# Threshold attention and an MLP mixer on one core: scores of two units per visit in six PSUM banks, everything else in two

## The chip, the cores and the metric

The kernel runs on 1 core of one Trainium2 chip. The metric is the device time of one execution in microseconds (us). Engines are named as in the profile: PE is TensorE (PEld its weight loads), DVE is VectorE, ACT is ScalarE, POOL is GpSimd, SP is SyncE, which here only issues DMAs. ACT issues DMAs as well, from the same instruction queue that it computes from. PSUM is the memory that PE writes to, eight banks of 128 partitions x 512 fp32 values.

## What is computed

```
batch, heads, seq, head_dim = 8, 8, 576, 64      d_model 512, d_tok 256, d_ch 1536, all fp32
scores = q @ k.T / 8
thresh = max(scores, -1) - tau                    (tau 0.02)
scores = where(scores >= thresh, scores, -1e9)
attn   = softmax(scores)                          (+1e-9 in the denominator)
x      = attn @ v, heads side by side             (8, 576, 512)
u      = x + (relu(x^T @ w_tok1) @ w_tok2)^T      mixing of tokens
out    = u + relu(u @ w_ch1) @ w_ch2              mixing of channels
```

The inputs come as 64-bit words where they are float64; the weights are converted to fp32 on the chip.

## The kernel before

**Units.** The attention of one batch row (called a row here, b = 0 to 7) has four pairs of heads. Two pairs make nine units of 128 queries each (the fifth shares its partitions between both pairs), so a row has UB = 18 units, and the program 144. A unit goes through: `scores` (L311: for each head of the pair two matmuls of 288 keys; they write a tile `sc` of two banks per head), a maximum per head on DVE (L316), the bias from it on POOL (L317), then `weigh`: the threshold as a Prelu on ACT out of PSUM (L326, "the mask" below) and the exponential with its sum in place (L333); then `norm`: 1/sum on DVE (L340, L341) and the multiplication on POOL (L344); then, two units later, `turn_blocks`: one 32x32-block transpose on DVE (L372), and after every third unit sixteen DMAs on SP that put the blocks in their places (L381, `eT<-T`). `values` (L416, L421: 20 or 40 matmul records into one bank, copied out by ACT at L425) follows three units after the third unit. Row 0 uses PE transposes through PSUM (`turn`, L360) in place of the blocks and DMAs.

**Loads.** q and k of the next pairs come in by DMAs on ACT's queue from row 1 on (`load_qk`, L109). The buffers `lq` and `lk` exist once. A load may start when `prep` (L293, two DVE block transposes, `qT<-lq` and `kT<-lk`) has read the pair before. `prep` stands at units t = 2 and 7 of every nine, the loads that follow it at t = 3, 4, 5, 6 and at 8, 0, 1, so at least one unit later.

**The MLP.** When a row's last values are done, `push(b)` puts its steps into the list `todo`: five transposes of x (`turn_x`, L450, copied out by ACT at L451), two `tok1` (L457, Relu on ACT at L459), eight `tok2` (L467, added to x on DVE at L471), and for each 256 tokens twelve `ch1` (L510, Relu on ACT at L511) and eight `ch2` steps (L531, four parts that add up in one bank for 128 tokens, then an add on DVE at L543 and the store at L550). Every step has a cost in the planner's us. `fill(share)` is called five times per unit and lets so much work out as a share of `quota`, the row's sum less KEEP (20, 45 for the last but one row) over 17 units. What is kept is done in the next row, between the first steps of that row. Rows 1 to 6 do half of their channel MLP in this way, and the rest is spilled and done at the end, as row 7's, by a product of seven block multiplications (`class Late`, L834) over five groups.

**PSUM.** `ps_sc` has two tiles of two banks (the two heads of one unit); `ps_tr` two banks for transposes and values; `ps_mm` two banks, from row 1 on, for `tok1`, `tok2`, `ch1` and `ch2`. In row 0 a third `sc` tile, `ps_3rd`, takes the place of `ps_mm`.

**Weights.** 31 pieces are loaded by SP into four raw buffers in turn and converted in steps by ACT (L206, L208), DVE (L216, L218, L222) and POOL (L230). `weight(n)` lets n of 94 steps out; `need(i)` lets out all up to piece i. In row 1 a unit has 9 steps, 12 as long as row 0's transposes are left.

The order on each engine is that in which the Python program writes the instructions; each engine runs its own in that order.

```
            if t == 2:
                prep(n + 1)
            if t == 7:
                prep(n + 2)
```

These lines stand after the loads of the same unit.

Of the kernel before, what the change touches and what calls it, by code (L numbers as in the profile page):

```python
# [21 lines left out]
def kernel(  # L22
# [52 lines left out]
    ps_sc = attn.enter_context(tc.tile_pool(name="ps_sc", bufs=2, space=bass.MemoryType.PSUM, side="right"))  # L75
    dram = ctx.enter_context(tc.tile_pool(name="dram", bufs=1, space=bass.MemoryType.DRAM))
    ps_tr = ctx.enter_context(tc.tile_pool(name="ps_tr", bufs=2, space=bass.MemoryType.PSUM))


    late = ctx.enter_context(ExitStack())  # L80
    ps_3rd = late.enter_context(tc.tile_pool(name="ps_3rd", bufs=1, space=bass.MemoryType.PSUM))
    ps_mm = None
# [65 lines left out]
    scratch = att.tile([P, GU * 4 * NK * 32], U32, tag="eT", name="scratch")  # L148
    extra = const.tile([P, 2 * WMAX], U32, name="extra")
    NRAW = 4  # L150

    high = work.tile([P, GR // P, 4, NCC * 32], F32, tag="ut", bufs=1, name="high").rearrange("q n a x -> q (n a x)")
    raw_at = [scratch[:, 2 * WMAX * i : 2 * WMAX * (i + 1)] for i in range(NRAW - 1)] + [extra]
# [28 lines left out]
    def load_piece(i):  # L182
        if i >= len(pieces):
            return
        dst, src = pieces[i]
        rows = dst.shape[0]
        n = 1
        for d in dst.shape[1:]:
            n *= d
        raw = raw_at[i % NRAW][0:rows, 0 : n * (2 if wide(i) else 1)].bitcast(src.dtype)  # L190
        nc.sync.dma_start(out=like(raw, dst), in_=src)
        if wide(i):
            words = raw.bitcast(U32).rearrange("p (n w) -> p n w", w=2)
            h2 = high[0:rows, WMAX * (i % 2) : WMAX * (i % 2) + n]
            raws[i] = like(words[:, :, 0], dst), like(words[:, :, 1], dst), like(h2, dst)
        else:
            raws[i] = like(raw, dst)
# [149 lines left out]
    def turn(u, third):  # L347
# [9 lines left out]
        ps = ps_tr.tile([P, MAIN], F32, tag="tr", name=f"tr{third}_{u}")[:, 0 : 3 * P].rearrange("p (c x) -> p c x", c=3)  # L357
# [40 lines left out]
    def values(b, p0, g):  # L398

        if b not in xTs:  # L400
            xTs[b] = work.tile([P, NP, S], F32, tag="xT", name=f"xT_{b}")
        eT = eTs.pop((b, p0, g))
        whole = ps_tr.tile([P, MAIN], F32, tag="tr", name=f"pv_{b}_{p0}_{g}")
# [28 lines left out]
    def token_mlp(b, ps=range(NP)):  # L432
# [8 lines left out]
        def psum(name):  # L441
            return (ps_mm or ps_tr).tile([P, DM], F32, tag="mm" if ps_mm else "tr", name=name)

        def turn_x(t, n):
            M = MT[t]
            to = ps_tr.tile([P, MAIN], F32, tag="tr", name=f"tx_{b}_{t}_{ps[0]}")[0:M, 0 : n * L * P].rearrange("p (t c x) -> p t c x", t=n, c=L)
# [6 lines left out]
        def tok1(m):  # L453
            need(2)
            to = psum(f"t1_{b}_{m}_{ps[0]}")[:, 0 : P * L]
            for t in range(NT):
                nc.tensor.matmul(to, lhsT=w1[:, t, P * m : P * m + P], rhs=x_sb[:, t, cols], start=(t == 0), stop=(t == NT - 1))  # L457
            if ps_mm:
# [4 lines left out]
        def tok2(c, f):  # L463
            need(6)
            to = psum(f"t2_{b}_{c}_{f}")[:, 0:HS]
# [19 lines left out]
    def channel_mlp(b, uT, i):  # L485
# [17 lines left out]

        def ch1(j):
# [3 lines left out]
            ps = ps_mm.tile([P, GR], F32, tag="mm", name=f"c1_{b}_{i}_{j}")[:, 0:n]  # L508
# [3 lines left out]
            if j == 1:  # L512
                s["us"] = work.tile([P, GR // P, 4, NCC * 32], F32, tag="us", bufs=1, name=f"us_{b}_{i}")
                if b:
                    s["ut"] = work.tile([P, GR // P, 4, NCC * 32], F32, tag="ut", bufs=1, name=f"ut_{b}_{i}")
                    turn_u()

        def ch2(t, part):
            need(7 + NJ + 3 * part + 2)
            t0 = GR * i + P * t  # L520
            if part == 0:
                s["ps"] = ps_mm.tile([P, NCC, P], F32, tag="mm", name=f"c2_{b}_{i}_{t}")
# [16 lines left out]
            if part == 3:  # L539
                o = s["us"][:, t].rearrange("q a x -> q (a x)")  # L540
                if b:
                    move_u()
# [7 lines left out]
                nc.sync.dma_start(out=out[b, t0 : t0 + P, :], in_=o)  # L550
# [5 lines left out]
    def move_u():  # L556
        while moves:
            moves.popleft()()

# [15 lines left out]
    KEEP = 20.0  # L575
    KEEP_FIRST = 20.0
    KEEP_LAST = 45.0
    todo = deque()
    quota = 0.0
    credit = 0.0  # L580

    def fill(share):
        nonlocal credit
        credit += share * quota
        while todo and credit > 0:
            cost, step = todo.popleft()
            credit -= cost
            step()
        if not todo:
            credit = 0.0  # L590


    early = deque()

    def push(b):
        nonlocal quota
        uT = xTs[b]
# [6 lines left out]
        for i, step in enumerate(steps):  # L604
            n = 2 if i in waits else 1
            todo.extend(old[:n] + [step])
            del old[:n]
        todo.extend(old)
        if b < B - 1:
            todo.append((0.0, lambda: kept.append(b)))  # L610
        for i in range(NOW[b]):
            todo.extend(channel_mlp(b, uT, i))
        quota = (sum(c for c, _ in todo) - (KEEP_FIRST if b == 0 else KEEP_LAST if b == B - 2 else KEEP)) / (UB - 1)
# [28 lines left out]
    for u in range(len(units) + LAG + 5):  # L642
        on = u < len(units)
        if u == UB:
            late.close()
            ps_mm = ctx.enter_context(tc.tile_pool(name="ps_mm", bufs=2, space=bass.MemoryType.PSUM))
        if on:
            b_now, p0, t = units[u]
            n = b_now * NP + p0
        w = u - LAG  # L650
        back = 0 <= w < len(units)
        if on:
            scores(u)
# [3 lines left out]
        if due and not in_blocks(due[0][1]):  # L657
# [4 lines left out]
        if 0 < u <= len(units):  # L662
# [3 lines left out]
        turns_left = b_now and back and not in_blocks(units[w][0])  # L666
        if b_now:
            if turns_left:
                weigh(u)
            else:  # L670
                weight(3)
        else:


            weight_to(2.25 * (u - (1 if visit else 1.5)))
            if visit:
                weigh(u)
        while copies:
            copies.popleft()()
        if last and u < UB:  # L680
            early.extend(token_mlp(0, range(NP // 2))[0])
        elif last:
            push(0)
        if back:
            wb, wp, wt = units[w]
            if not in_blocks(wb):
                for i in range(3):
                    turn(w, i)
            if wt % GU == GU - 1:
# [3 lines left out]
                due.append((u + (3 if in_blocks(wb) else 1), wb, wp, g))  # L693
        if b_now:
            fill(0.4)
        if back and in_blocks(wb):
            turn_blocks(w)
        if b_now:
            weight(6 if turns_left else 3)
        if turns_left:  # L700
            fill(0.6)
        elif on and (b_now or not visit):
            weigh(u)
        elif b_now:
            fill(0.6)
        if b_now:
            weight(3)
        elif u == 0:
# [4 lines left out]
        if on:  # L713


            when = {3: (2, 0, 2), 4: (2, 2, 4), 5: (2, 4, 6), 6: (2, 6, 8), 8: (3, 0, 3), 0: (1, 3, 6), 1: (1, 6, 8)}
            if u == 0:
                load_qk(1, (nc.sync, nc.sync), range(0, 3))
            if t in when:
                m, lo, hi = when[t]  # L720
                if n + m < len(pairs):
                    load_qk(n + m, (nc.scalar if b_now else nc.sync,) * 2, range(lo, hi))
            if t in (3, 7) and n + 2 + t // 4 < len(pairs):
                load_v(n + 2 + t // 4)
            if t == 2:
                prep(n + 1)
            if t == 7 and n + 2 < len(pairs):
                prep(n + 2)
        if due and in_blocks(due[0][1]):
            values_due(u)  # L730

        if back and wt % GU == 0 or not on:
            move_u()
# [278 lines left out]
```

## Time and profile before

| | us |
|---|---|
| median of 3 runs (1410.24 to 1419.52) | 1413.34 |
| the profiled execution | 1407.55 |
| its span | 1405.8 |
| PE busy | 1290.4 (92%) |
| DVE, ACT, POOL busy | 734.3, 592.9, 374.7 |
| unit 18, the first of row 1, starts its scores | 99.2 |
| unit 126, the first of row 7 | 837.9 |
| first matmul of the last stage (L834) | 1031.6 |

A row of the profile's groups gives busy time and the mean of one instruction, then the idle time of the engine just before such instructions and what ended it. An fp32 matmul stands there as two records. "PEclk" and "granted clock" are the share of TensorE's full clock that was granted; matmuls take longer in proportion.

### The profile page before, as it was taken

Reading aid. Unit: us, or ns where it says so; the run is one execution under the profiler, and the core shown is the slowest. Engines: PE = TensorE matmul, PEld = TensorE weight load, DVE = VectorE, ACT = ScalarE, POOL = GpSimd, SP = SyncE. Lnnn points to the kernel's source line nnn. Section 1 sums busy time; section 2 is a strip of 40 time slices with the busy share of each in tenths; the row PEclk is TensorE's granted clock in tenths of the full one; section 3 lists DMA queues with packets and bytes.
Section 4 is the critical chain, followed back from the end, with each engine's and each line's share of the span. In section 5 each row is a group of like instructions: output and inputs, shape, how many; then the busy total and the mean of one; then the engine's idle time right before and its main releaser. Section 6 shows DMA issues by size and latency. Waiting matters only on the chain.

```text
span 1405.8 us, 18371 instructions
## 1 busy us (share of the span) xinstructions
PE 1290.4 (92%) x6190; PEld 866.9 (62%) x6190; DVE 734.3 (52%) x1297; ACT 592.9 (42%) x1285; POOL 374.7 (27%) x710
## 2 busy tenths in 40 slices
PE   7886599999799989999998998898989999999998
PEld 5554365645554655564474465446658888888887
DVE  6879755446555645655564464554134443434342
ACT  6766454455555645555454454561111110202020
POOL 4565533233333323333333232330000101010100
PEclk8998899999999999999999999999999999999999
DMA  6535645646776676567566667645011110121011
GB/s 118 124 88 145 177 98 128 133 102 146 139 145 143 130 158 127 130 137 151 127 137 131 136 142 144 132 101 136 6 47 29 60 31 31 30 60 31 31 30 30
DMA packets 310574, 144.90 MB, mean 103 GB/s; under 512 B 210065, under 2 KB 303249, under 8 KB 310481
## 3 DMA queue, kind: packets, MB, share of 16 engines
q1 hardware_dynamic: 182768, 127.84, 39.1%
q10 hardware_dynamic: 127712, 15.90, 7.4%
q8 instruction: 49, 0.80, 0.3%
q14 instruction: 45, 0.36, 0.1%
HBM read 47.32 MB, written 13.50 MB: 43 GB/s over the span
## 4 chain that ended last, share of the span: by engine, by line
PE 80%; DVE 6%; DMA 5%; SPq 4%; ACT 2%; issue 1%; POOL 1%; ACTq 0%; DVEq 0%; POOLq 0%
PE c L531 11%; PE sc L311 11%; PE c L510 10%; PE o L834 9%; PE pv L421 8%; PE hx L834 6%; PE t L457 4%; PE t L467 4%; PE hz L834 4%; PE oz L834 4%; PE hmm L834 4%; PE pv L416 3%; SPq L381 2%; DMA eT<-T 2%; DVE mx L316 2%; DMA lq<-in_q_dram 1%
## 5 line engine op out<-in xcount | busy, mean ns | idle before, releaser
L316 DVE TENSOR_REDUCE mx<-sc 128x1 f32<-128x576 f32 x288 | 204.6, 750 | 331.5 <-PE sc L311 330.3
L326 ACT ACTIVATE e<-sc,bias 128x576 f32<-128x576 f32 x288 | 200.4, 740 | 135.3 <-POOL bias L317 128.3
L311 PE MATMUL sc<-kT,qT 64*128 64x288 f32 (+1 forms) x1280 | 206.5, 441 | 32.4 <-ACT e L326 31.3
L317 POOL TENSOR_SCALAR bias<-mx,toff 128x1 f32<-128x1 f32 x288 | 82.2, 286 | 565.9 <-DVE mx L316 510.0
L333 ACT ACTIVATE e<-e,ntau 128x576 f32<-128x576 f32 x288 | 220.8, 772 | 0.0
L344 POOL TENSOR_SCALAR e<-e,rr 128x576 f32<-128x576 f32 x288 | 216.5, 765 | 12.9 <-DVE rr L341 2.0
L510 PE MATMUL c<-xT,wc 128*128 128x256 f32 x768 | 182.7, 390 | 10.2 <-ACT g L511 9.1
L311 PEld LDWEIGHTS sc<-kT,qT 64*128 64x128 f32 (+1 forms) x1280 | 112.8, 180 | 124.8 <-ACT e L326 62.2
L531 PE MATMUL c<-wc,g 128*128 128x512 f32 x384 | 178.0, 604 | 0.0
L372 DVE STREAM_TRANSPOSE T<-e 128x1152 f32<-128x1152 f32 x126 | 172.0, 1365 | 7.2 <-DMA eT<-T 3.4
L510 PEld LDWEIGHTS c<-xT,wc 128*128 128x128 f32 x768 | 144.2, 193 | 46.9 <-issue 15.2
L421 PE MATMUL pv<-eT,lv 128*64 128x384 f32 (+1 forms) x1024 | 144.1, 424 | 0.0
L915 POOL TENSOR_TENSOR us<-us,ut 128x256 f32<-128x256 f32 x27 | 22.4, 845 | 411.6 <-DVE us L756 411.6
L531 PEld LDWEIGHTS c<-wc,g 128*128 128x128 f32 x384 | 70.1, 193 | 76.5 <-issue 75.9
L421 PEld LDWEIGHTS pv<-eT,lv 128*64 128x64 f32 x1024 | 79.4, 144 | 55.4 <-issue 49.7
L467 PE MATMUL t<-w,a 128*128 128x288 f32 x256 | 75.1, 431 | 10.7 <-DVE xT L471 10.7
L425 ACT COPY xT<-pv 128x384 f32<-128x384 f32 (+1 forms) x56 | 21.0, 400 | 136.6 <-PE pv L421 125.4
L416 PE MATMUL pv<-eT,vl 128*64 128x384 f32 (+1 forms) x256 | 49.5, 459 | 30.6 <-DMA eT<-T 29.5
L457 PE MATMUL t<-x_sb,w 128*128 128x512 f32 (+1 forms) x180 | 75.1, 565 | 0.0
L511 ACT ACTIVATE g<-c 128x256 f32<-128x256 f32 x96 | 36.8, 383 | 87.0 <-PE c L510 80.0
L467 PEld LDWEIGHTS t<-w,a 128*128 128x128 f32 x256 | 46.9, 194 | 36.1 <-DVE xT L471 16.8
L880 ACT ACTIVATE ga<-hmm 128x256 f32<-128x256 f32 x30 | 11.5, 384 | 123.6 <-PE hmm L834 123.6
(111 smaller groups left out, 1523.5 us busy)
## 6 DMA issues: line engine op xcount, KB each, us to landing
eT<-T SPq DMA_DIRECT2D x672, 108.0 KB, 2.3
lv<-in_v_dram SPq DMA_DIRECT2D x32, 288.0 KB, 4.0
scratch<-in_moe_w_ch_dram SPq DMA_DIRECT2D x18, 512.0 KB, 4.1
out_dram<-us SPq DMA_DIRECT2D x32, 256.0 KB, 2.0
ut<-us SPq DMA_DIRECT2D x256, 32.0 KB, 1.9
lk<-in_k_dram ACTq DMA_DIRECT2D x109, 72.0 KB, 3.1
lq<-in_q_dram ACTq DMA_DIRECT2D x106, 72.0 KB, 2.5
spill<-xT SPq DMA_DIRECT2D x6, 640.0 KB, 4.1
```

Source lines behind the costliest of these rows:

```text
L311: nc.tensor.matmul(sc[h][rows, f, 0:HS], lhsT=qT[r, cols], rhs=kT[r, HS * f : HS * f + HS], start=True, stop=True)
L316: nc.vector.tensor_reduce(out=mx[:, c], in_=sc[h][:, :, 0:HS], axis=AX.XY, op=ALU.max)
L326: nc.scalar.activation(out=eh, in_=sc[h][:, :, 0:HS], func=AF.Prelu, bias=bias[:, h : h + 1], scale=SCALE, alpha=STEEP)
L333: nc.scalar.activation(out=eh, in_=eh, func=AF.Exp, bias=ntau, accum_out=rs[:, h : h + 1])
L344: nc.gpsimd.tensor_scalar(out=eh, in0=eh, scalar1=rr[:, h : h + 1], scalar2=1.0, op0=ALU.mult, op1=ALU.mult)
L372: nc.vector.transpose(out=T[:, :, place, :].rearrange("p a (c x) -> p c a x", c=NK), in_=e.rearrange("p (c a x) -> p c a x", c=NK, a=4))
L421: nc.tensor.matmul(to[r], lhsT=lv[:, j, :], rhs=e[j], start=False, stop=(c == NI - 1), skip_group_check=True)
L457: nc.tensor.matmul(to, lhsT=w1[:, t, P * m : P * m + P], rhs=x_sb[:, t, cols], start=(t == 0), stop=(t == NT - 1))
L467: nc.tensor.matmul(to, lhsT=a[:, m, P * c : P * c + P], rhs=w2[:, m, HS * f : HS * f + HS], start=(m == 0), stop=(m == NTK - 1))
L510: nc.tensor.matmul(ps, lhsT=wc1[:, j, c, :], rhs=uT[:, c, GR * i : GR * i + n], start=(c == 0), stop=(c == NCC - 1))
L531: nc.tensor.matmul(flat, lhsT=s["g"][:, j, P * t : P * t + P], rhs=wc2[:, j, :], start=(j == 0 and b > 0), stop=(j == NJ - 1), skip_group_ ...
L834: nc.tensor.matmul(ps, lhsT=l, rhs=r, start=start and x == 0, stop=x == len(pairs) - 1, skip_group_check=not start)
```

## The change

Row 0 is kept as it was, in a loop of its own. After it all its PSUM pools are closed, and the other rows run in rounds of two units. The scores of both units go to two tiles of three banks (one per head), so that each bank holds 192 keys of the first unit and 192 of the second; 12 matmuls of 192 columns take the place of two times four of 288. All other users share the two banks left, in turn; a bank in which a `ch2` is adding up is skipped. The masks of both units now come before their exponentials, with MLP steps let out between them. The values come at the end of a round, two rounds after their unit. `prep` now stands ahead of the loads of the same unit, and the loads of both units stand ahead of the first mask. `fill` fills up to a share of a round's `quota`, in which scores (2.35) and values (4.2) are counted; `finish` does what is left of the row two before. Weights have three raw buffers in other places and seven steps a round in row 1. Stores of results are issued at the start of the next round. In the last stage, sums of weights and inputs are moved ahead, between the last steps of the rows.

```diff
+    def bank(name, hold=False):
+        if not banks:
+            return ps_tr.tile([P, MAIN], F32, tag="tr", name=name)
+        turn_of = (turn_of + 1) % len(banks)
+        if turn_of == held:
+            turn_of = (turn_of + 1) % len(banks)
+        if hold:
+            held = turn_of
+        pool, tag = banks[turn_of]
+        return pool.tile([P, MAIN], F32, tag=tag, name=name)
...
-    NRAW = 4
+    NRAW = 3
...
-            ps = ps_mm.tile([P, GR], F32, tag="mm", name=f"c1_{b}_{i}_{j}")[:, 0:n]
+            ps = bank(f"c1_{b}_{i}_{j}")[:, 0:n]
...
-                s["ps"] = ps_mm.tile([P, NCC, P], F32, tag="mm", name=f"c2_{b}_{i}_{t}")
+                s["ps"] = bank(f"c2_{b}_{i}_{t}", hold=True).rearrange("q (c d) -> q c d", c=NCC)
...
-                nc.sync.dma_start(out=out[b, t0 : t0 + P, :], in_=o)
+                stores.append(lambda: nc.sync.dma_start(out=out[b, t0 : t0 + P, :], in_=o))
...
-    KEEP = 20.0
-    KEEP_FIRST = 20.0
-    KEEP_LAST = 45.0
+    KEEP = 12.0
+    KEEP_LAST = 22.0
+    SCORES, VALUES = 2.35, 4.2
+    ROUNDS = UB // 2
...
+    def fill(to):
+        nonlocal spent
+        while todo and spent < to * quota:
+            cost, step = todo.popleft()[0:2]
+            spent += cost
+            step()
...
+    row0.close()
+    pairing = attn.enter_context(tc.tile_pool(name="ps_s2", bufs=2, space=bass.MemoryType.PSUM, side="right", reuse_waits="tile"))
+    ps_b = ctx.enter_context(tc.tile_pool(name="ps_b", bufs=1, space=bass.MemoryType.PSUM, reuse_waits="tile"))
+    banks.extend([(ps_b, "m0"), (ps_b, "m1")])
+    HT = S // 3
+
+    def scores_of_two(us):
+        sc = [pairing.tile([P, 3, MAIN], F32, tag="sc", name=f"sc{h}_{us[0]}") for h in range(2)]
+        for k, u in enumerate(us):
...
+            for f in range(3):
+                for n, cols, rows in parts:
+                    for h in range(2):
...
+                            sc[h][rows, f, HT * k : HT * k + HT],
...
+        for k, u in enumerate(us):
...
+                nc.vector.tensor_reduce(out=mx[:, c], in_=part[h], axis=AX.XY, op=ALU.max)
+                nc.gpsimd.tensor_scalar(out=bias[:, c], in0=mx[:, c], scalar1=toff, scalar2=-SCALE, op0=ALU.add, op1=ALU.mult)
...
+    def loads(u):
+        b, p0, t = units[u]
+        n = b * NP + p0
+        if t == 2:
+            prep(n + 1)
+        if t == 7 and n + 2 < len(pairs):
+            prep(n + 2)
+        when = {2: (2, 0, 3), 3: (2, 3, 6), 4: (2, 6, 8), 7: (3, 0, 3), 8: (3, 3, 6), 0: (1, 3 if u == UB else 6, 8)}
+        if t in when:
+            m, lo, hi = when[t]
+            if n + m < len(pairs):
+                load_qk(n + m, (nc.scalar,) * 2, range(lo, hi))
...
+    for it in range(rounds + 2):
...
+        if on:
+            scores_of_two(us)
+            spent += SCORES
+        if 0 < it <= rounds:
+            turned(us[0] - 1)
+        store()
+        spill()
+        move_u(8)
+        if on:
+            for u in us:
+                loads(u)
+            if b_now == 1:
+                weight(3)
+            mask(us[0])
...
+            fill(0.33)
+            mask(us[1])
+            fill(0.48)
+            exps(us[0])
+            fill(0.63)
+            norm(us[0])
+            if b_now == 1:
+                weight(2)
+            exps(us[1])
+            fill(0.8)
+            norm(us[1])
+            turned(us[0])
+            if b_now == 1:
+                weight(2)
+        if visit:
+            fill(1.0 - VALUES / quota)
+            _, b, p0, g = due.popleft()
+            values(b, p0, g)
...
+            spent += VALUES
+            if p0 == NP - 2 and g == 2:
+                push(b)
+        fill(1.0)
+        spent = max(spent - quota, 0.0)
```

`mask` and `exps` are the two halves of the former `weigh`; `turned` is `turn_blocks` with the entry of the group's values into `due`.

## Prediction, on record before the run

> **What bounds the kernel now.** First the page: busy times by engine and the costliest groups.
>
> ```profile
> PE 1290.4 (92%) x6190; PEld 866.9 (62%) x6190; DVE 734.3 (52%) x1297; ACT 592.9 (42%) x1285; POOL 374.7 (27%) x710
> ...
> L316 DVE TENSOR_REDUCE mx<-sc 128x1 f32<-128x576 f32 x288 | 204.6, 750 | 331.5 <-PE sc L311 330.3
> L326 ACT ACTIVATE e<-sc,bias 128x576 f32<-128x576 f32 x288 | 200.4, 740 | 135.3 <-POOL bias L317 128.3
> ```
>
> PE is busy for 92%, and DVE and ACT wait for it. Next the stretches between the first scores of rows 2, 6 and 7 and of their successors, to see what there is to win:
>
> ```profile
> 258.50:371.30 112.80, 105.16 (x513) 58.26 (x512) 63.53 (x109) 59.77 (x130) 37.30 (x80) 0.97 0.60 128
> 716.80:837.90 121.10, 113.03 (x545) 64.82 (x545) 65.41 (x110) 63.15 (x138) 39.06 (x82) 0.96 0.63 134
> 837.90:953.20 115.30, 98.45 (x465) 52.79 (x464) 61.98 (x102) 62.37 (x135) 39.13 (x82) 0.92 0.63 129
> ```
>
> The second figure is the stretch, the third PE's busy time in it. Rows 2 to 7 take 112.6 to 121.1 us each and leave PE idle for 6 to 17 us; some clock is lost as well. That, and 28 us in row 1, is all that can be won. Then the timeline of row 3, for durations:
>
> ```profile
> 502.91 1.37 ACT L326 ACTIVATE e<-sc,bias 128x576 f32<-128x576 f32 x2
> ...
> 504.25 1.31 PE L311 MATMUL sc<-kT,qT 64*128 64x288 f32 x8
> ...
> 504.60 0.74 DVE L293 STREAM_TRANSPOSE kT<-lk 128x576 f32<-128x576 f32 x1
> ...
> 505.50 3.72 PE L510 MATMUL c<-xT,wc 128*128 128x256 f32 x16
> 505.52 1.42 DVE L316 TENSOR_REDUCE mx<-sc 128x1 f32<-128x576 f32 x2 [0.19 <-PE sc L311]
> ...
> 505.68 0.38 ACT L511 ACTIVATE g<-c 128x256 f32<-128x256 f32 x1
> ...
> 507.14 1.36 DVE L372 STREAM_TRANSPOSE T<-e 128x1152 f32<-128x1152 f32 x1
> ```
>
> Last, row 1, for what a wait on ACT does to PE:
>
> ```profile
> 169.42 0.65 ACT L206 ACTIVATE scratch<-scratch 128x512 int32<-128x512 uint32 x1 [10.14 <-DMA scratch<-in_moe_w_ch_dram]
> ...
> 170.52 0.37 ACT L511 ACTIVATE g<-c 128x256 f32<-128x256 f32 x1
> ...
> 170.94 3.41 PE L510 MATMUL c<-xT,wc 128*128 128x256 f32 x8 [9.13 <-ACT g L511]
> ```
>
> One ACT instruction stood for 10.14 us; the Relu behind it was late, and PE, which had both banks for `ch1` full, stood for 9.13. A wait at the head of ACT's queue goes straight into PE as soon as two banks are full. Half a clock followed: 8 records took 3.41, where 16 take 3.72.
>
> **The change, part by part.**
>
> *Scores.* Two units took 2 x 1.3 = 2.6 us of PE. The new 12 matmuls (24 records in pairs) cost 2.25 if their columns set the pace (192 for 288, plus 0.3 to start) and 2.65 if a weight load of 0.19 for each pair does. PEld's 0.19 is longer than the 0.16 of 192 columns, so 2.6: no gain. The low end is worth at most 63 x 0.35 = 22 us, if every round ended with PE.
>
> *The wait of scores for masks* (PE sc <- ACT e, 31.3 us in all) goes, as the two tiles are long read when PE comes round. *The wait of values for `eT<-T`* (29.5 us) goes too: values come two rounds later. So up to 60 us are there.
>
> *Where the reduces begin.* In the program as built the first reduce waits for the semaphore that the last of the 12 matmuls sets: 2.7 us into a round, 1.3 after a unit's first matmul before.
>
> *Loads ahead of the masks.* This is the step that decides. In DVE's order of the built program a round is: four reduces (2.84), the transpose of the unit before (1.36), in four of nine rounds `qT` and `kT` (1.48), later 1/sums and the next transpose. On ACT the loads stand first, then the masks; the first load waits for this round's `qT`, as `lq` exists once. In before the loads stand a unit later, and the masks' idle time put down to a load of k is 4.7 us in the whole run. So in these rounds ACT stands still until 2.7 + 2.84 + 1.36 + 1.48 = 8.4 us; three or six loads (0.49 apart at 717.5) end at 9.3 or 10.7. Masks that could start at 3.9 start 5.4 or 6.8 us late. Queued behind: masks, exponentials, every Relu and copy out of PSUM; waiting for those: PE. Once started, two masks twice (2.74) and four exponentials (3.2) follow, then 1/sum and a transpose on DVE before the next reduces: a chain of 14.6 us plus 0.35 per Relu, against 9.0 in the other rounds. PE has 105 / 9 = 11.7 to do.
>
> *Two banks for all else.* `ch1`, `tx`, `tok1`, `tok2` and values had four banks, now two, and one while a `ch2` adds up. PE's order by rounds in row 5, units 90 to 106 by twos, with before's durations (`ch1` 1.73, a `ch2` part 2.6, `tx` 0.43, `tok1` 4.4, `tok2` 1.07, values 3.4): 13.8, 11.2, 8.7, 14.7, 10.8, 10.2, 14.8, 11.2, 9.5, sum 105; so planned rounds are not equal. Laid out by hand, the last one (loads of six, four `ch1`): scores to 2.6, two `ch1` to 6.1, both banks full; masks 10.7 to 13.5, first Relu at 13.85, third `ch1` to 15.6; the second Relu stands behind two exponentials, at 15.8; fourth `ch1` to 17.6. Work 9.5, round 17.6. In the same way the nine take 13.8, 12.9, 14.0, 20.1, 15.1, 19.3, 18.1, 13.8, 17.6, sum 144.7. What is late in each: 94, the first `tx` has the bank of a `ch2` whose add on DVE stands behind late reduces (10.4 for 5.2); 96, a `tx` whose bank is copied behind held masks (12.8 for 8.2), then values behind an add; 98, `tok1` behind the last copy (7.3 for 3.0); 100, `tok2` behind a Relu behind held masks (12.8 for 7.0), then a bank whose add stands behind sums and a transpose (18.2 for 15); 102, five adds one by one. Bounds per row: 123 if PE never waits for a bank (four rounds of 15.5, the others at the longer of their work and about 10), 153 if each stall also halves the clock. I take 145 for rows 3 to 6, nearest to the 9.13 row, where a held ACT was felt by PE nearly in full.
>
> *Clock.* The granted clock by stretches of 5 us:
>
> ```profile
> 866.00:871.00 5.00, 0.76 (x4) 0.42 (x6) 0.00 (x0) 0.95 (x4) 0.64 (x3) 0.92 1.11 208
> 871.00:876.00 5.00, 5.00 (x26) 2.33 (x24) 0.00 (x0) 0.48 (x1) 0.00 (x0) 0.74 0.91 170
> 876.00:881.00 5.00, 4.43 (x19) 1.78 (x16) 3.58 (x6) 2.88 (x6) 2.00 (x4) 1.00 0.45 91
> 881.00:886.00 5.00, 3.59 (x13) 2.22 (x14) 4.16 (x9) 3.16 (x7) 2.62 (x7) 0.78 0.55 104
> ```
>
> After 4.65 us without PE the next 5 us ran at 0.74, and around 1.98 idle (880.4 to 882.4) at 0.78: 1.3 and 1.1 us lost. Six stalls a row make 8 us; part of it falls where ACT sets the end, so it is the upper bound.
> The Trainium skill (TensorE: Matmul & The Clock Gate, Part 1) gives half clock after an idle window of about 3.4 us until 3.4 us of work; by it a stall of 4 us or more would cost 1.7, one of 2 us mostly nothing, and the row's loss would be about 8 too. The 1.98 us here already cost clock, so the row counts. The rule speaks against this change, which makes few long stalls out of many short ones.
>
> *Row 1.* 159.3 before. PE's work is 133. Three raw buffers and seven steps a round leave eight pieces of weights for one round (unit 28): each takes DVE about 1.6 to 2.1 (L216, L218, L222), so 13 to 17 us ahead of that round's 1/sums; and in the second round `tok1`'s Relu stands behind two rounds' masks and weights. From 161 (only the four load rounds longer) to 195 by the hand layout; 185, as these waits are hard ones. *Row 2*: work 96, 118 to 135, taken 130. *Row 7 and the rest of the steps*: 193.7 before; 156 of work (less was kept back), stalls of 10 to 22, so 172. *Last stage*: 374.2 before, less the wait of hx for DVE t (4.58): 369. SP: stores and moves come later in its queue and nobody waits for them; POOL's order is unchanged.
>
> **Sum:** 99.2 + 185 + 130 + 4 x 145 + 172 + 369 = 1535, for a span of 1405.8. The profiled execution is 1.75 above its span and 5.8 below the median of the runs shown: 1535 + 8 = 1543, rounded to 1540.
>
> **Rivals.**
>
> 1. *ACT is held, PE is not.* PE runs ahead on `ch2` parts, which need no copy, and rows take 123. For it: half of the steps are `ch2`. Against: order between steps is fixed. 99 + 165 + 125 + 4 x 123 + 170 + 369 + 8 = 1428.
> 2. *Faster.* DVE reaches `qT` and `kT` before the masks could start anyway, because PE, no longer waiting for masks, gives scores early and DVE (52% busy) is ahead. Then loads cost nothing, rounds are PE's work and a row takes 110: 99 + 155 + 105 + 440 + 165 + 369 + 8 = 1341. Point of decision: the transposes end by 3.9 us into a round. Against it: DVE's own order puts 2.84 + 1.36 ahead of them after scores.
> 3. *As forecast, and the clock is lost in full*: 8 us more in each of six rows, 1590.
>
> That the plan does what it says is already answered by PE's order: rounds hold 3.0 to 20.2 us of work.
>
> **How the numbers follow.** Forecast 0.50, rival 1 0.20, rival 2 0.12, rival 3 0.18. Within 1% (1399 to 1427; a measurement of this kernel can't tell less from no change) lies the lower part of rival 1: 0.08. Faster by more: 0.12. Slower: 0.80. The range reaches from rival 1 to rival 3, 1420 to 1605, and leaves out rival 2 and the outermost part of the others. The forecast's own is 1490 to 1590 (rows of 135 to 153).
>
> **What would show it.** Right: ACT's `lq` issues end at 8 to 11 us after the start of four rounds in nine, with idle ACT before, and PE idle for 4 to 8 us in `ch1`, `tx` or `tok2` of the same rounds; rows 3 to 6 at 135 to 153 with granted clock under 0.95; waits of scores for masks gone; the last stage near 369. Wrong: first masks at 4 us in all rounds; `ch1` waiting for less than 2 us; rows under 125. Scores at 2.3 a round would show that columns, not weight loads, set their pace.

## The result, and the profile after

The changed kernel takes 1621.0 us, median of four runs (1616.9 to 1621.2), the one before 1412.6 in the same session: ratio 1.146 (95% interval 1.142 to 1.150). The forecast was slower, 1540 with a range of 1420 to 1605: the direction and the wait that decides were right, the size was too small. Two profiled executions among the experiments (runs 2 and 7) had a lower clock than the timed ones: lengths read from run 2 are some 2% long, and nothing is read from run 7's trace.

The page of the kernel after, busy times and the groups that answer to those of before:

```profile
PE 1334.0 (82%) x6750; PEld 932.4 (58%) x6750; DVE 745.4 (46%) x1297; ACT 584.7 (36%) x1285; POOL 371.9 (23%) x710
...
L778 ACT ACTIVATE e<-sc,bias 128x576 f32<-128x576 f32 x252 | 168.8, 741 | 383.8 <-DVE mx L768 120.8
L768 DVE TENSOR_REDUCE mx<-sc 128x1 f32<-128x576 f32 x252 | 172.9, 748 | 181.6 <-PE sc L754 181.6
L527 PE MATMUL c<-xT,wc 128*128 128x256 f32 x768 | 199.0, 417 | 66.8 <-ACT g L528 63.9
```

Work of ACT, DVE and POOL is the same to 11 us. PE, 92% busy before, is at 82%. ACT stands for 383.8 us ahead of its masks (135.3 before), and `ch1` stands for 63.9 us for a Relu (9.1 before). By stages, from the first scores of each row (the fourth column is the same kernel with its loads put behind the exponentials, the first experiment below):

| us | before | predicted | after | after, loads behind |
|---|---|---|---|---|
| up to row 1 | 99.2 | 99.2 | 102.1 | 99.2 |
| row 1 | 159.3 | 185 | 212.1 | 195.1 |
| row 2 | 112.8 | 130 | 143.9 | 125.4 |
| rows 3 to 6, each | 116.6 | 145 | 148.4 | 123.0 |
| row 7 and rest of the steps | 193.7 | 172 | 199.7 | 188.1 |
| last stage | 374.2 | 369 | 367.7 | 367.6 |
| span | 1405.8 | 1535 | 1619.1 | 1467.3 |

The program up to row 1 is nearly the same in all versions, and that stage takes 98.8 to 102.3 in the profiles, so 3 us there mean nothing.

The timeline of one round with six loads (row 5, units 106 and 107; start and length in us, engine, line; in brackets the idle time before and what ended it):

```profile
885.36 2.22 PE L754 MATMUL sc<-kT,qT 64*128 64x192 f32 x24
...
887.51 3.72 PE L527 MATMUL c<-xT,wc 128*128 128x256 f32 x16
887.61 2.75 DVE L768 TENSOR_REDUCE mx<-sc 128x1 f32<-128x576 f32 x4 [5.79 <-PE sc L754]
...
890.28 1.37 DVE L388 STREAM_TRANSPOSE T<-e 128x1152 f32<-128x1152 f32 x1
...
891.57 0.73 DVE L309 STREAM_TRANSPOSE qT<-lq 128x576 f32<-128x576 f32 x1
892.23 0.74 DVE L309 STREAM_TRANSPOSE kT<-lk 128x576 f32<-128x576 f32 x1
892.34 0.32 ACTq L123 DMA_DIRECT2D lq<-in_q_dram  x1
...
895.00 0.51 ACTq L123 DMA_DIRECT2D lk<-in_k_dram  x1
895.62 2.63 ACT L778 ACTIVATE e<-sc,bias 128x576 f32<-128x576 f32 x4 [9.66 <-DMA lq<-in_q_dram]
898.12 0.40 ACT L528 ACTIVATE g<-c 128x256 f32<-128x256 f32 x1
...
898.58 5.12 PEld L527 LDWEIGHTS c<-xT,wc 128*128 128x128 f32 x16 [7.74 <-ACT g L528]
898.58 5.52 PE L527 MATMUL c<-xT,wc 128*128 128x256 f32 x16 [7.34 <-ACT g L528]
```

Read from the top: reduces, transpose and prep follow one another on DVE; the first load goes out 0.04 us after `qT` is done (892.30); the sixth is out at 895.5, and only then the masks start, 10.3 us into the round; behind them comes the Relu that frees a bank. PE had both banks full at 891.2 and stands for 7.34. The next 16 records then take 5.52 where the same 16 took 3.72. In the 5 us stretches of this round the clock (the last column but two) shows why:

```profile
885.40:890.40 5.00, 5.00 (x39) 4.46 (x38) 2.79 (x5) 0.48 (x1) 0.80 (x3) 1.00 0.63 135
890.40:895.40 5.00, 0.83 (x4) 0.38 (x2) 2.57 (x3) 0.00 (x0) 0.26 (x1) 1.00 0.30 50
895.40:900.40 5.00, 1.82 (x4) 1.51 (x5) 0.30 (x2) 4.78 (x11) 0.00 (x0) 0.50 0.92 184
900.40:905.40 5.00, 5.00 (x29) 4.11 (x29) 1.72 (x4) 2.17 (x6) 2.93 (x4) 0.81 0.26 65
```

In rows 3 to 6 PE's idle time (the stretch less the busy time) went from 32.4 to 127.1 us, and its busy time, for the same steps, from 434.2 to 466.6, as the granted clock went from 0.97 to 0.88.

### The profile page after: what moved, and what is told of

It reads as the page before. It is cut to its first block, busy times and chain, and to the rows that moved or that the text cites. A ratio compares the mean times of both kernels' runs of the same rounds, so it can differ in the third digit from the quotient of the medians.

```text
span 1619.1 us, 19579 instructions
## 1 busy us (share of the span) xinstructions
PE 1334.0 (82%) x6750; PEld 932.4 (58%) x6750; DVE 745.4 (46%) x1297; ACT 584.7 (36%) x1285; POOL 371.9 (23%) x710
## 4 chain that ended last, share of the span: by engine, by line
PE 57%; DVE 15%; ACT 14%; DMA 6%; issue 4%; ACTq 2%; SPq 2%; POOL 0%; DVEq 0%; POOLq 0%
PE o L965 8%; PE c L527 7%; DVE mx L768 7%; ACT e L778 6%; PE c L548 6%; PE pv L438 5%; PE sc L754 5%; PE hx L965 5%; ACT e L785 4%; DVE T L388 4%; PE t L481 4%; PE oz L965 3%; PE hmm L965 3%; PE hz L965 3%; PE t L471 2%
## 5 line engine op out<-in xcount | busy, mean ns | idle before, releaser
L778 ACT ACTIVATE e<-sc,bias 128x576 f32<-128x576 f32 x252 | 168.8, 741 | 383.8 <-DVE mx L768 120.8
L768 DVE TENSOR_REDUCE mx<-sc 128x1 f32<-128x576 f32 x252 | 172.9, 748 | 181.6 <-PE sc L754 181.6
L527 PE MATMUL c<-xT,wc 128*128 128x256 f32 x768 | 199.0, 417 | 66.8 <-ACT g L528 63.9
L527 PEld LDWEIGHTS c<-xT,wc 128*128 128x128 f32 x768 | 157.0, 209 | 104.0 <-ACT g L528 59.8
L548 PE MATMUL c<-wc,g 128*128 128x512 f32 x384 | 197.8, 659 | 16.9 <-POOL wc L246 16.6
L785 ACT ACTIVATE e<-e,ntau 128x576 f32<-128x576 f32 x252 | 193.3, 783 | 0.0
L388 DVE STREAM_TRANSPOSE T<-e 128x1152 f32<-128x1152 f32 x126 | 172.1, 1366 | 11.7 <-POOL e L360 6.5
L356 DVE TENSOR_SCALAR rr<-rs 128x2 f32<-128x2 f32 x144 | 35.6, 247 | 307.6 <-ACT e L785 307.6
L754 PE MATMUL sc<-kT,qT 64*128 64x192 f32 (+1 forms) x1680 | 153.7, 344 | 11.3 <-ACT e L778 10.9
L481 PE MATMUL t<-w,a 128*128 128x288 f32 x256 | 92.5, 516 | 63.1 <-ACT a L473 24.2
L481 PEld LDWEIGHTS t<-w,a 128*128 128x128 f32 x256 | 59.3, 242 | 94.5 <-DVE xT L485 27.9
L464 PE MATMUL tx<-ident,xT 128*128 128x128 f32 (+1 forms) x160 | 28.7, 312 | 50.2 <-ACT x_sb L465 39.7
L471 PEld LDWEIGHTS t<-x_sb,w 128*128 128x128 f32 x180 | 34.6, 201 | 51.9 <-issue 32.2
```

The source lines that it names most:

```text
L388: nc.vector.transpose(out=T[:, :, place, :].rearrange("p a (c x) -> p c a x", c=NK), in_=e.rearrange("p (c a x) -> p c a x", c=NK, a=4))
L481: nc.tensor.matmul(to, lhsT=a[:, m, P * c : P * c + P], rhs=w2[:, m, HS * f : HS * f + HS], start=(m == 0), stop=(m == NTK - 1))
L527: nc.tensor.matmul(ps, lhsT=wc1[:, j, c, :], rhs=uT[:, c, GR * i : GR * i + n], start=(c == 0), stop=(c == NCC - 1))
L548: nc.tensor.matmul(flat, lhsT=s["g"][:, j, P * t : P * t + P], rhs=wc2[:, j, :], start=(j == 0 and b > 0), stop=(j == NJ - 1), skip_group_ ...
L754: nc.tensor.matmul(sc[h][rows, f, HT * k : HT * k + HT], lhsT=qT[r, cols], rhs=kT[r, HT * f : HT * f + HT], start=True, stop=True, skip_gr ...
L768: nc.vector.tensor_reduce(out=mx[:, c], in_=part[h], axis=AX.XY, op=ALU.max)
```

## The experiments

Each ratio is to the kernel before on the same chip, with its 95% interval.

**1. Loads behind the exponentials.** Theory A is the prediction's: ACT is held at the head of its queue. Theory B: two banks are too few for everything else, whoever is held.

```diff
             for u in us:
-                loads(u)
+                preps(u)
...
             exps(us[1])
+            for u in us:
+                loads(u)
```

> The kernel after, with one step moved: the loads of q, k and v of both units are issued behind the last exponential of the round, no longer ahead of its first mask; prep stays where it is. Theory A (the loads at the head of ACT's queue hold the masks, and PE stands behind them with two banks full): masks start 4.5 to 5 us into every round, the waits of ch1 for Relu (63.9 us in all) and of tx for copies (39.7) fall to under half, rows 3 to 6 take 118 to 128 us each where the kernel after takes 148.4, row 1 some 195 to 205 (its weights stay), and the time is 1450 to 1500. Theory B (two banks for everything else are too few, whoever is held): rows stay at 138 to 148, the time is 1560 to 1615, and the waits of PE stay with the same lines.

Measured: 1473.0 us, ratio 1.044 (1.039 to 1.049). This one step is worth 148 us of the 208 by which the change is slower. Masks start at 4.5 to 5 us in all but 12 of the 63 rounds. The same round as above:

```profile
782.51 2.67 ACT L778 ACTIVATE e<-sc,bias 128x576 f32<-128x576 f32 x4 [3.86 <-DVE mx L768]
...
785.06 0.39 ACT L528 ACTIVATE g<-c 128x256 f32<-128x256 f32 x1
...
785.35 0.32 ACTq L123 DMA_DIRECT2D lq<-in_q_dram  x1
785.50 1.59 PEld L527 LDWEIGHTS c<-xT,wc 128*128 128x128 f32 x8 [1.98 <-ACT g L528]
785.50 3.77 PE L527 MATMUL c<-xT,wc 128*128 128x256 f32 x16 [1.57 <-ACT g L528]
```

The wait for the Relu is 1.57 where it was 7.34, the 16 records behind it take 3.77, and the round 11.1 where it took 18.7. Theory A holds, B is out as the main cause. From row 1 to the last stage PE stands idle for 156 us where the kernel after has 262, and loses 51 us to the clock where that has 94 (how this is counted is told further below): so of the 148 us some 105 are idle PE and 43 are clock.

**2. The loads' part alone, in the kernel before** (`loads` as in the change, prep first; the old place is left to row 0).

```diff
         elif on and (b_now or not visit):
+            if b_now:
+                loads(u)
             weigh(u)
...
-        if on:
+        if on and not b_now:
```

> The kernel before with one part of the change alone: prep and, right behind it, the loads of the same unit stand ahead of that unit's mask. Theory A (the hold alone is enough): in the units with a prep ACT stands 3 to 4 us more, twice a row, rows 2 to 6 grow by 5 to 9 us and the time is 1440 to 1475. Theory B (a hold of ACT only hurts where everything else has two banks): rows grow by less than 2 us, 1412 to 1425.

Measured: 1484.7, ratio 1.051 (1.046 to 1.056). More than either theory said: 75 us with all four banks in place. A unit with a prep there:

```profile
587.77 1.36 DVE L372 STREAM_TRANSPOSE T<-e 128x1152 f32<-128x1152 f32 x1
...
589.05 0.73 DVE L293 STREAM_TRANSPOSE qT<-lq 128x576 f32<-128x576 f32 x1
...
589.82 0.32 ACTq L109 DMA_DIRECT2D lq<-in_q_dram  x1
...
591.51 1.37 ACT L326 ACTIVATE e<-sc,bias 128x576 f32<-128x576 f32 x2 [8.05 <-DMA eT<-T]
...
592.87 1.34 PE L311 MATMUL sc<-kT,qT 64*128 64x288 f32 x8
```

ACT is idle for 8.05 us, the first load again goes out behind `qT`, and here it is the next scores that wait for the mask (the brackets name the DMA that landed last; in ACT's queue the load stands ahead of the mask). All waits of scores before, and in this run:

```profile
L311 PE MATMUL sc<-kT,qT 64*128 64x288 f32 (+1 forms) x1280 | 206.5, 441 | 32.4 <-ACT e L326 31.3
```

```profile
L311 PE MATMUL sc<-kT,qT 64*128 64x288 f32 (+1 forms) x1280 | 231.6, 465 | 83.8 <-ACT e L326 81.8
```

The hold needs no shortage of banks to hurt: with four banks for everything else it comes out at the scores' own banks.

**3. The two banks alone, in the kernel before** (transposes, MLP and values in two banks in turn; the banks set free stay empty).

```diff
-        ps = ps_mm.tile([P, GR], F32, tag="mm", ...)
+        ps = bank(f"c1_{b}_{i}_{j}")
```

> The kernel before with one other part alone: from row 1 on transposes, token and channel MLP and values share two PSUM banks in turn (one while a ch2 adds up); the two banks set free are left empty, scores keep their four. Theory A (banks only hurt behind a held ACT): rows grow by 0 to 5 us, 1412 to 1450. Theory B (two banks are too few in themselves): rows grow by 15 to 30 us, 1510 to 1620.

Measured: 1421.9, ratio 1.009 (1.006 to 1.011). Rows 3 to 6 take 117.4 each, 116.6 before. Theory A.

**4. Loads left ahead of the masks, prep a round earlier.** Is it the wait or the issuing?

```diff
     def loads(u):
-        if t == 2:
-            prep(n + 1)
-        if t == 7 and n + 2 < len(pairs):
-            prep(n + 2)
...
             norm(us[0])
+            for u in us:
+                if u + 2 < len(units):
+                    preps(u + 2)
```

> The kernel after with the loads left ahead of the masks, but prep moved to a round earlier (behind 1/sum of its first unit), so that no load finds itself ahead of the transpose it waits for. Theory A (what held ACT is the wait of the first load for this round's prep, 8.5 us into the round; the issues themselves, 6 x 0.49 = 2.9 us, end before masks can start): masks start 4.5 to 5 us into nearly all rounds of rows 3 to 6, rows take 118 to 127, row 1 195 to 205, the time is 1450 to 1500, as with the loads put behind. Rival A2 (it is the issuing itself, with its own waits for earlier transfers, that holds ACT wherever it stands ahead of masks): masks stay at 8 us and more in the rounds with loads, rows above 135, the time above 1540.

Measured: 1498.5, ratio 1.062 (1.057 to 1.066); rows 3 to 6 took 128.7 each. One of its rounds with six loads, units 88 and 89:

```profile
670.79 2.22 PE L754 MATMUL sc<-kT,qT 64*128 64x192 f32 x24
671.03 0.35 ACTq L123 DMA_DIRECT2D lq<-in_q_dram  x1
...
673.90 0.51 ACTq L123 DMA_DIRECT2D lk<-in_k_dram  x1
...
675.24 2.67 ACT L778 ACTIVATE e<-sc,bias 128x576 f32<-128x576 f32 x4 [3.87 <-DMA lk<-in_k_dram]
```

Six loads are out 3.6 us into the round and the masks start at 4.45, as they do without loads: here issuing six DMAs ahead of them costs nothing, the wait for this round's prep did. So it is in five of the eight rounds with six loads in rows 3 to 6; in the other three a later load waits too, and the masks start at 5.0 to 6.3. The time lies in theory A's range, the rows 2 us above theirs. The 25 us that it is over run 1 lie mostly in prep's new place, as the next run shows.

**5. Prep last, loads behind.** On the kernel of run 1:

```diff
-            for u in us:
-                preps(u)
             mask(us[0])
...
             norm(us[0])
+            for u in us:
+                preps(u)
```

> The kernel with the loads behind (1473.0), and prep moved from the round's start to behind 1/sum of its first unit, still ahead of the loads that need it. Theory D (tok2 waits on DVE for its add to x behind four reduces, a transpose and, in four of nine rounds, prep: 14.1 us in rows 3 to 6): the adds start 1.5 us earlier in those rounds, rows get 1 to 2.5 us shorter and the time is 1455 to 1468. Rival (prep at the end is late for the loads, and these hold ACT at the start of the next round): rows 1 to 4 us longer, 1478 to 1505.

Measured: 1492.2, ratio 1.058 (1.054 to 1.062): the rival's time, with rows 3 to 6 at 127.9 each, 5 us longer and not 1 to 4. Loads behind the late prep end 3 us later (13.4 us into the round of unit 88, 10.4 in run 1), and `ch1` waits for Relus behind them, at the end of the same round (2.7 us each in the rounds of units 88 and 124). Runs 4 and 5 overlap in their intervals: with prep that late, no difference can be told between loads on either side of the masks.

**6 and 7. What is left in rows 3 to 6.** On the kernel of run 1: the first step ahead of both masks (6, first diff); transpose and prep behind the first step on DVE (7, second).

```diff
-            mask(us[0])
             fill(0.33)
+            mask(us[0])
             mask(us[1])
```

```diff
-            turned(us[0] - 1)
-            for u in us:
-                preps(u)
             mask(us[0])
             fill(0.33)
+            turned(us[0] - 1)
+            for u in us:
+                preps(u)
             mask(us[1])
```

> The kernel with the loads behind (1473.0), and the steps that stood between the first and the second unit's masks put ahead of both. Theory C (what is left in rows 3 to 6, 59.8 us of idle PE in four rows against 33.5 before, is mostly PE waiting for a Relu or a copy behind the masks, as there are only two banks): a Relu goes out at 4.3 us, ahead of the masks, the waits for ch1's Relu and for tx's copies fall from 28 to under 15 us in rows 3 to 6, these take 118 to 121 (now 123.0), and the time is 1440 to 1460. Rival (the first step ends after the masks could start, 4.5 us, and holds masks and exponentials instead): rows 123 to 128, 1473 to 1500.

> The kernel with the loads behind (1473.0), and on DVE the transpose of the unit before and prep moved from right behind the four reduces to behind the first step of the round. Theory D' (the wait of tok2 for its adds, 14.1 us in rows 3 to 6, and part of tx's wait for an add, 5.5, are DVE's block of four reduces, a transpose and prep, 5.7 us at the head of a round): those waits fall by half, rows 3 to 6 get 2 to 3 us shorter and the time is 1450 to 1464. Rival (the wait only goes on to the values and loads, which come behind the later transposes): 1468 to 1490.

Measured: 1470.9, ratio 1.043 (1.039 to 1.047), and 1476.9, ratio 1.046 (1.041 to 1.051). Both theories fall: neither order moves the time by more than the measurement tells. In run 6 rows 3 to 6 took 121.6 each for 123.0, and the waits for Relus and copies there fell from 28 to 24 us, not to under 15.

**8, 9, 10. Weights in row 1.** The kernel after with 6 + 6 + 6 steps a round for 3 + 2 + 2 (8); the kernel of run 1 with two steps in each of nine places (9), and with 3 + 2 + 2 in two rounds and 19 a round from the third on (10). The kernel before lets nine steps out in every unit of row 1, the first ones too (3 + 3 + 3, or 6 + 3 as long as row 0's transposes are left), so 18 in two units. The diff of (8); `weight(2)` is put between the other parts of the round in the same way in (9) and (10).

```diff
-                weight(3)
+                weight(6)
             mask(us[0])
...
-                weight(2)
+                weight(6)
             exps(us[1])
```

> The kernel after with 6 + 6 + 6 steps of the weights in each round of row 1 in place of 3 + 2 + 2. Theory A' (the 45.2 us round of unit 28 is eight pieces of weights let out in one place, through three raw buffers): row 1 falls from 212 to 180 to 190 us, the round of unit 28 to about 20, the first rounds grow by 1 to 3 us each, all other rows stay within 1 us, and the time is 1590 to 1600. Rival (the sum of the weights' work on DVE, ACT and POOL sets row 1, wherever it stands): row 1 stays above 205, the time above 1612.

> The kernel with the loads behind (1473.0), and in row 1 the weights two steps at a time in nine places of a round (18 a round, as in the run with 6 + 6 + 6, where the whole got longer, and as many as before had in two units), in place of 3 + 2 + 2. Theory E (the place decides: in bursts of six, ACT stands for two loads of raw pieces in turn, 6 to 15 us; spread, each load has some 4 us to land): row 1 falls from 195 to 168 to 182, the round of unit 28 from 43 to under 22, the time is 1445 to 1462. Rival (three raw buffers and loads of 3.2 us each behind SP's eT<-T set the pace wherever the steps stand): row 1 stays at 188 to 205, the time at 1466 to 1485.

> The kernel with the loads behind (1473.0), in row 1 with 3 + 2 + 2 steps of the weights in the first two rounds, and from the third on two more in each of six places, 19 a round. Theory E' (from the run with two by two: the burst in the round of unit 28, 43 us, goes if the steps come earlier, and the 12 to 13 us that the first two rounds lost there don't come back if these keep their seven steps): row 1 takes 160 to 172 us, and the time is 1436 to 1452. Rival (what the third to fifth rounds then let out costs as much as the burst): row 1 over 180, the time over 1458.

Measured: 1640.3, ratio 1.162 (1.158 to 1.166); 1460.5, ratio 1.037 (1.033 to 1.042); 1474.3, ratio 1.045 (1.040 to 1.050). Row 1 took 232.8 (for 212.1), 181.6 and 191.6 (for 195.1): the rival in runs 8 and 10, theory E in run 9, at the edge of its range. The burst in the round of unit 28 went in all three (45.2 and 43.2 us to 16.7), and came back in the second to fourth round. From run 10, its fourth round:

```profile
179.51 10.28 SPq L397 DMA_DIRECT2D eT<-T  x16
...
190.56 0.58 SPq L207 DMA_DIRECT2D spare<-in_moe_w_ch_dram  x1
...
194.54 0.65 ACT L222 ACTIVATE spare<-spare 128x512 int32<-128x512 uint32 x1 [18.84 <-DMA spare<-in_moe_w_ch_dram]
195.09 1.35 ACT L778 ACTIVATE e<-sc,bias 128x576 f32<-128x576 f32 x2
196.34 0.38 ACT L528 ACTIVATE g<-c 128x256 f32<-128x256 f32 x1
...
196.87 3.75 PE L527 MATMUL c<-xT,wc 128*128 128x256 f32 x8 [17.79 <-ACT g L528]
```

It is the same hold once more: a conversion at the head of ACT's queue stands 18.84 us for its piece, and mask, Relu and PE stand behind it. The piece's DMA itself went out only at 190.56, as sixteen issues of `eT<-T` stood ahead of it in SP's queue until 189.79: a hold behind a hold. Only spreading in twos gained (12 us; its interval and run 1's just overlap, and row 1's 13.5 us speak for it).

**11. Three raw buffers alone, in the kernel before** (`NRAW = 3`).

> The kernel before with three raw buffers for the weights in place of four, all else as it was. Row 1 took 159.3 us there and 195.1 in the changed kernel with its loads put behind. Theory F (the third part of row 1's growth is the missing raw buffer: each piece's load is awaited at the head of ACT's queue one piece earlier): row 0 and row 1 together grow by 15 to 35 us, rows 2 to 7 by less than 1, the time is 1425 to 1445. Rival (the number of buffers does little; it is where and in which portions the steps stand): rows 0 and 1 grow by less than 8 us, 1408 to 1420.

Measured: 1423.3, ratio 1.008 (1.005 to 1.011); the start and row 1 took 1.9 and 9.0 us more, together 10.9, between the two theories. The 1.9 are within the start's own variation. In that order of work the buffer makes 9 of the 36 us by which row 1 of run 1 is longer than before.

**12, 13, 14. The useful parts alone, in the kernel before.** The sums of inputs ahead of the last stage (12), values one unit later (13), both (14).

```diff
+    sums.extend(lambda n=n: lates[0].sum_u(n) for n in range(4))
...
-                due.append((u + (3 if in_blocks(wb) else 1), wb, wp, g))
+                due.append((u + (4 if in_blocks(wb) else 1), wb, wp, g))
```

> The kernel before with the last stage's four sums of inputs ahead of its first matmul, as the change has them. If its wait for them (4.58 us of PE, and the clock after it) is all that the change gains in the last stage: 1404 to 1409, the last stage 368 to 370 us long where it was 374.2. If other work of DVE takes that place: 1409 to 1414.

> The kernel before with one part of the change alone in its smallest form: values one unit later (four units after the third of their group, no longer three). If the wait of values for eT<-T (29.5 us of idle PE) goes and nothing takes its place, rows 2 to 7 get 3 to 5 us shorter and the time is 1383 to 1398. If the DMAs of the next group now wait for the eT that is read a unit later, or PE then waits for masks instead: 1405 to 1420.

> The kernel before with both small edits, the sums of the last stage ahead (1401.7 alone, ratio 0.994) and values one unit later (1407.7 alone, ratio 0.998). If they add up: ratio 0.990 to 0.993, 1396 to 1400. If the later values are worth nothing: 1400 to 1403, as the sums alone.

Measured: 1401.7, ratio 0.994 (0.992 to 0.997); 1407.7, ratio 0.998 (0.995 to 1.000); 1400.3, ratio 0.993 (0.991 to 0.995). The last stage of run 12 is 368.1 us long, 374.2 before, and its wait is gone (first line before, second run 12):

```profile
L834 PE MATMUL hx<-t,w1s 128*128 128x256 f32 x120 | 31.7, 388 | 4.6 <-DVE t L759 4.6
```

```profile
L834 PE MATMUL hx<-t,w1s 128*128 128x256 f32 x120 | 30.8, 379 | 0.0
```

Values one unit later gain nothing that can be told: their wait for `eT<-T` is 30.1 us there, 29.5 before. Both edits together can't be told from the sums alone. These two versions with the sums ahead (12 and 14) are the only ones that are faster than the kernel before beyond the noise, by less than 1%.

## Why the prediction was right and where it failed

*Loads ahead of the masks: right.* In rows 3 to 6 the issues of six loads end 10.1 to 11.7 us into their rounds and masks start right behind them; 10.7 had been worked out. The figure is that close in part by luck: in most of these rounds the first load went out at 7.0, behind `qT` alone, and not at 8.4 behind both transposes, and six of them took 3.2 us and not 2.3. Runs 1, 2 and 4 show the cause. The condition of rival 2 (transposes by 3.9 us into a round) was not met: they end at 7.6 at the earliest. Rival 1 fell with PE's 127.1 us of idle time.

*Rounds by hand: right in sum, by two errors that cancel.* Row 5 took 14.1, 12.3, 14.5, 20.7, 12.1, 19.5, 18.4, 15.9, 18.7, sum 146.1, where 13.8, 12.9, 14.0, 20.1, 15.1, 19.3, 18.1, 13.8, 17.6, sum 144.7, had been laid out. But the layout held no clock. Row 5 has 30.7 us of idle PE and 115.4 of busy, against 105 of work and 40 of stalls in the layout: stalls were laid out some 9 us too long and the clock took that much.

*Waits to go: right.* From row 1 on, values no longer wait for `eT<-T` (29.5 us before), and scores wait 10.9 us for masks (28.7). But values now wait 20.6 us for a bank whose add or copy on DVE is late.

*Two banks, and the last stage: right.* Banks alone cost 12 us (run 3); the last stage took 367.7 for 369.

*Scores: wrong, but against the direction of the miss.* Two units take 2.22 us at full clock (median of 45 visits of run 1), not 2.6; two of before take 2 x 1.24. So there is a gain, of about 63 x 0.26 = 16 us of PE's time. I had set 0.19 per weight load against 0.16 of columns, but 24 loads of 0.187 each took 1.93 in all: they overlap, and columns set the pace.

*The failed step is the clock, which the sum put at nothing.* The forecast's terms for rows 1 to 7 were PE's work and PE's stalls; a loss of clock stood only in the bound of 153 and in rival 3, at 8 us in each of six rows, because part of it was expected to fall where ACT sets the end anyway. The traces let the three be told apart: what PE's busy time would be at full clock (each piece of it times the granted clock at that moment), what is busy beyond that, and what is idle. ("Set" under stalls is what the forecast's term holds beyond its work.)

| us | work: set, came | stalls: set, came | clock: set, came | sum: set, came |
|---|---|---|---|---|
| row 1 | 133, 125.8 | 52, 61.2 | 0, 25.1 | 185, 212.1 |
| row 2 | 96, 94.2 | 34, 37.5 | 0, 12.2 | 130, 143.9 |
| rows 3 to 6 | 420, 418.6 | 160, 127.1 | 0, 48.0 | 580, 593.7 |
| row 7 and rest | 156, 154.6 | 16, 35.9 | 0, 9.2 | 172, 199.7 |
| together | 805, 793.2 | 262, 261.7 | 0, 94.5 | 1067, 1149.4 |

Of the 84 us by which the sum of 1535 was short, the clock is more than all: 94.5 (32.5 in the same stages of the kernel before), less 12 of work. That the stalls agree in sum is luck: 33 us too many in rows 3 to 6, 33 too few in the others. The steps of rows 3 to 6 need 418.7 us at full clock in run 1 too, where the clock was 0.97, so the two counts agree.

*Second, the stalls of row 1 and of row 7 and the rest were set too short.* In row 1 the hold costs 17 us; without it (run 1) the row takes 195.1, more than the 185 that I had with it. In its second round PE stands 16.3 us for a copy of values on DVE that comes behind 1/sums, a transpose and weights; and the eight pieces let out for unit 28 had been counted at DVE's 1.6 to 2.1 us each. They come in a chain from ACT over DVE to POOL, every 2.8 us (starts on POOL 234.20, 237.10, 239.58, 242.48, 245.53, 248.42), and PE takes them one by one at half clock:

```profile
237.10 1.34 POOL L246 TENSOR_TENSOR wc<-wc 128x512 int32<-128x512 int32 x1 [1.60 <-DVE wc L238]
...
238.49 2.07 PE L548 MATMUL c<-wc,g 128*128 128x512 f32 x2 [0.87 <-POOL wc L246]
...
239.58 1.29 POOL L246 TENSOR_TENSOR wc<-wc,extra 128x512 int32<-128x512 int32 x1 [1.14 <-DVE wc L238]
...
240.93 2.07 PE L548 MATMUL c<-wc,g 128*128 128x512 f32 x2 [0.36 <-POOL wc L246]
```

That round took 45.2 us. In row 2 the hold costs 18.5 and in row 7 and the rest 11.6; without it row 7 and the rest still take 188.1, with 25.2 us of idle PE where 16 had been set with the hold.

*The range failed with it.* Its upper end had rival 3's 8 us of clock in six rows, 48 in all; these rows lost 69, at 12 each in rows 3 to 6, and row 1, which had no clock in any case, lost 25. Row 1's own bound of 195 was passed by 17.

*Open.* With the loads behind, the kernel is still 63 us slower than before: 36 in row 1, 13 in row 2, 25 in rows 3 to 6, less 12 at the end and in row 7. PE does some 20 us less work than before (16 of it the scores), but stands 70 us longer and loses 18 more to the clock. Two banks (12 us) and three raw buffers (11) alone don't make that up, and runs 6 and 7 did not find the 25. The idle time there (59.8 us in four rows, 32.4 before) lies in some forty waits of up to 4.4 us, for adds of `tok2` (14.1), Relus (13.8) and copies of x (14.1). That rounds of two units give four masks and four reduces in one block, with two banks to bridge them, is argued, not shown; the new order of the steps (`quota`, KEEP) was not tested apart either.

## What to carry to other kernels

An instruction that waits at the head of an engine's queue costs what stands behind it, so a DMA issue on a computing engine belongs behind the engine's urgent work or behind a wait that is long over; six issues without a wait cost nothing in most rounds here, the same ones behind a wait cost 148 us in the whole run. Price every such hold at nearly its length, and the clock on top: in rows 3 to 6 masks started 22 us later per row than in run 1, PE stood 17 us longer per row and lost 9 more to the clock. A stage with one-off work (here row 1 with its weights) needs its own sum over the whole chain of engines, not one engine's share of it.

## What the runs showed of the hardware

*The clock.* In 14 profiles (all but those of runs 2 and 7) the granted clock has two values, 1.0 and 0.5, and changes only at times that lie a multiple of 3.413 us apart, to within 1 ns in each profile. So each profile can be cut into windows of 3.413 us, and each window looked at for how long PE was idle in it and which clock the next one had. Of the windows at full clock:

| PE idle in the window | windows | next one at half clock |
|---|---|---|
| under 20% | 4428 | 0 |
| 20 to 40% | 388 | 14 |
| 40 to 50% | 163 | 22 |
| 50 to 60% | 95 | 55 |
| over 60% | 261 | 261 |

And of the windows at half clock, the next was at full clock in 322 of 340 with PE idle for under 10%, in 29 of 72 with 10 to 20%, and in 1 of 248 with more. So a window in which PE is idle for more than about half is followed by one at half clock, which costs 1.7 us of work; and at half clock 0.7 us of idle time in a window are enough to keep the next one there. Whether a wait of 1.5 to 3.4 us loses anything depends on how it falls across two windows: past the first 300 us, the longest wait that stood alone and lost nothing took 3.39 us. This fits with rows 3 to 6, which lost 12 us each where the prediction had counted six stalls at 1.3.

The Trainium skill (TensorE: Matmul & The Clock Gate, Part 1) gives the half clock after an idle window of about 3.4 us that runs freely. The length of the window and of the loss agree with these traces. That the whole window has to be idle does not: over 60% of one was enough in every case, and 50 to 60% in more than half.

*Weight loads overlap*: 24 of 0.187 us each in 1.93 us, as told above.
